# Block cross-attention into a gated FFN on one core: x kept head-major, a block-diagonal state operand, cast loads, and one batch's transpose on the DMA crossbar

## The chip, the cores and the metric

The kernel runs on one core of one Trainium2 chip. A core has a matrix engine (TensorE, PE in the profile), a vector engine (VectorE, DVE), a scalar engine (ScalarE, ACT), a general one (GpSimd, POOL) and a sync engine (SyncE, SP) that only issues transfers. Each engine executes its own instructions in order and waits for others by semaphores. Sixteen DMA engines move data. The metric is the device time of one execution in microseconds (us); lower is better.

## The reference: what is computed

For each of 8 batches and 8 heads there are 512 rows of x and 32 rows of state, 64 wide. The two attend to each other, and the result, 544 rows per batch with the heads side by side (512 wide), goes through a gated FFN with 1536 hidden units.

```
scores  = x @ state^T / 8;        a  = softmax(scores);   xread = a @ state     # 512 x 64 per head
scores2 = state @ x^T / 8;        a2 = softmax(scores2);  sread = a2 @ x        # 32 x 64 per head
z   = concat(xread, sread) per head, heads side by side                          # 4352 x 512
out = (relu(z @ w_gate) * (z @ w_val)) @ w_out                                   # 4352 x 512, f32
```

## The kernel before, in words

Work is in bf16 with f32 sums in PSUM. PSUM has eight banks of 128 x 512 f32; the program assigns them by hand.

**Folding.** xread is never formed. For each batch `u_unit` (in 512-wide pieces) or `c_unit` (in 128- or 256-wide pieces) multiplies state into w_gate and w_val (line 303), and ACT and DVE copy the products U from PSUM (313, 323). `gv` (328) multiplies U by the transposed, normalised weights `ans` and gives both FFN branches for 128 hidden units and 512 rows. ACT makes the relu of one (352), DVE multiplies it by the other (356) into h, and `out_part` (365) multiplies h by w_out. ACT copies the result out (373) and SP stores it (377). The 256 rows of sread go through `gvs` (345) at the end.

**Attention.** x of one batch lies with 128 row groups in the partitions, 4 rows (c) to each group. It is transposed so that 64-wide heads stand in partitions. A block of `xT` holds two heads of one c. State is converted into `st_b` with two copies, of which each keeps every other group of rows by a multiplication with 0 or 1 (`odd`, `state_conv`); transposed, this gives `stT`, 64 columns for each pair of heads, with each head's 32 columns zero in the other head's rows. `att_sc` (209) multiplies a block of xT by these 64 columns: 8 matmuls for four heads. Then come exp on ACT (216), sum, reciprocal and scaling on DVE (222 to 228) and a transpose to `ans`, on PE for batches 0 and 1, and by the DMA crossbar from SP for the others (`att_aT_dma`, 236). For sread the unnormalised exp is multiplied by x padded with a column of ones (`x_pad` on POOL, 265; `sr_mm`, 273).

**How x comes in and is transposed.** Four heads of batch 0 are loaded in f32 by SP and ACT and converted; its other heads, batch 1 and batch 2 are loaded by casting DMAs on POOL's queue (427, 435). [...] Batches 0 to 2 are transposed on PE: whole blocks for the converted pairs (178), and half blocks, 64 columns each, in pairs for the rest (182, 195); ACT and DVE copy the result from PSUM (186, 198). From batch 3 on, x is loaded in f32 (`x_dma`, 105; batch 3 by POOL, the rest by SP), converted by POOL in two halves (151), and transposed by the crossbar from SP (`x_trans_dma`, 168).

**Order.** Up to the fourth hidden block of batch 2 the order is a hand-written list, `program`, each word one step on each of its engines: `dx.2.0.1` loads batch 2 by a cast, `c.0.1024.256@75` is c_unit of batch 0, columns 1024 to 1279, into banks 7 and 5, `co` its copies, `gv`, `re`, `mu` are gv, relu and multiplication, `xT2.2.0`/`xo2.2.0` transposes batch 2 and copies it, `stT.1`/`sto.1` does so for the state of batches 2 and 3, `sc`, `ex`, `nr`, `nx` are the attention, `ad` the crossbar transpose of a, `o.0.1` is out_part 1 of batch 0, `do` and `ds` load w_out and state. A step of the list that a DMA queue executes waits in that queue in this order too. After the list a loop runs gv of one block and an out_part eighteen blocks behind it, and `at(b, jf, ...)` hangs the other work on blocks: loads, transposes, attention of the next batch, U of the next batch, state transposes for batches 4 to 7 by the crossbar (`state_T_dma`, copied by ACT, 138).

**Buffers.** f32 x has two buffers (`xin`), bf16 x four, xT two, output rows (`o_sb`) four. At the end `out_last` (394, 397) divides the last 128 rows into four column pieces with a copy and a store each.

Of the kernel before, what the change touches and what calls it, by code (L numbers as in the profile page):

```python
# [8 lines left out]
FP32 = mybir.dt.float32  # L9
BF16 = mybir.dt.bfloat16  # L10
# [6 lines left out]
def kernel(  # L17
# [9 lines left out]
    nc = tc.nc  # L27
# [17 lines left out]
    xin = pool("xin", 2)  # L45
# [5 lines left out]
    opool = pool("opool", 4)  # L51
# [15 lines left out]
    odd = const.tile([128, 2], FP32, name="odd")  # L67


    stT = const.tile([128, B, NJ, 64], BF16, name="stT")  # L70
# [29 lines left out]
    def x_dma(b, engs):  # L100
        xf[b] = xin.tile([128, H, NC, D], FP32, name="xf", tag="xf")
        n = H // len(engs)
        for i, eng in enumerate(engs):
            src = x[b, i * n:(i + 1) * n].rearrange("h (p c) d -> p h c d", c=NC)
            eng.dma_start(out=xf[b][:, i * n:(i + 1) * n], in_=src)

    def xb_alloc(b):
        xb[b] = att.tile([128, NC * H * D], BF16, name="xb", tag="xb", bufs=4)
# [10 lines left out]
    def state_conv(g, half, eng):  # L119
        dst, src, keep = st_b[:, g % 3, :, half], st_f[:, g], odd[:, half:half + 1]  # L120
        if eng == "act":
            nc.scalar.activation(out=dst, in_=src, func=AF.Copy, scale=keep)
        else:
            e = {"dve": nc.vector, "pool": nc.gpsimd}[eng]
            e.tensor_scalar(out=dst, in0=src, scalar1=keep, scalar2=None, op0=ALU.mult)
# [11 lines left out]
    def state_out_dma(g, eng):  # L137
        copy[eng](out=stT[:, 2 * g:2 * g + 2].rearrange("p b j m -> p (b j m)").rearrange("p (q i m) -> p q i m", i=4, m=8),
                  in_=held["st", g].rearrange("p i (q m) -> p q i m", m=8))

    def state_out(g, eng):
        copy[eng](out=stT[:, 2 * g:2 * g + 2].rearrange("p b j m -> p (b j m)"), in_=held["st", g])

    def x_conv(b, half, eng):
        if b not in xb:
            xb_alloc(b)
            xb[b] = xb[b].rearrange("p (c h d) -> p c h d", c=NC, h=H)
        conv_heads(b, slice(HK * half, HK * half + HK), eng)

    def conv_heads(b, hs, eng):  # L150
        copy[eng](out=xb[b][:, :, hs].rearrange("p c h d -> p h c d"), in_=xf[b][:, hs])  # L151

    def x_conv_pair(b, j, eng):
        dst = x_head(b)[:, :, 2 * j:2 * j + 2].rearrange("p c h d -> p h c d")
        copy[eng](out=dst, in_=xf[b][:, 2 * j:2 * j + 2])

    def x_head(b):
        return xb[b][:, 0:NC * HK * D].rearrange("p (c h d) -> p c h d", c=NC, h=HK)

    def x_tail(b):  # L160
        return xb[b][:, NC * HK * D:].rearrange("p (h c d) -> p c h d", c=NC, h=HK)

    def xT_alloc(b):
        xT[b] = att.tile([128, NC, NJ, 128], BF16, name="xT", tag="xT")

    def x_trans_dma(b):
        xT_alloc(b)
        nc.sync.dma_start_transpose(out=xT[b].rearrange("p c j t -> p (c j) t"),
                                    in_=xb[b].rearrange("p c h d -> p (c h d)"))

    def x_T(b, j):

        if b not in xT:
            xT_alloc(b)
        ps = bank("xT_ps").bitcast(BF16)[:, 0:512].rearrange("p (c t) -> p c t", c=NC)
        for c in range(NC):
            if b == 0 and j < 2:
                nc.tensor.transpose(ps[:, c], x_head(b)[:, c, 2 * j:2 * j + 2].rearrange("p h d -> p (h d)"), id128)
            else:
                v, h = (x_tail(b), 2 * j - HK) if b == 0 else (xb[b], 2 * j)  # L180
                for h2 in range(2):
                    nc.tensor.transpose(ps[64 * h2:64 * h2 + 64, c], v[:, c, h + h2], id128)  # L182
        held["xT", b, j] = ps

    def x_out(b, j, eng):
        copy[eng](out=xT[b][:, :, j], in_=held["xT", b, j])  # L186

    def x_T2(b, half):
        if b not in xT:
            xT_alloc(b)  # L190
        ps = held["xT2", b, half] = bank("xT_ps").bitcast(BF16).rearrange("p (c j t) -> p c j t", c=NC, j=2)
        for j in range(2):
            for c in range(NC):
                for h2 in range(2):
                    nc.tensor.transpose(ps[64 * h2:64 * h2 + 64, c, j], xb[b][:, c, 4 * half + 2 * j + h2], id128)  # L195

    def x_out2(b, half, eng):
        copy[eng](out=xT[b][:, :, 2 * half:2 * half + 2], in_=held["xT2", b, half])


    def att_sc(b, jp):
        if b not in e_sn:
            e_sn[b] = att.tile([128, 2, NC, NJ * Ns], BF16, name="e_sn", tag="e_sn", bufs=4)
            a_sn[b] = att.tile([128, 2, NC, NJ * Ns], BF16, name="a_sn", tag="a_sn")
        t = held["sc", b, jp] = bank("sc_ps")
        ps = t.rearrange("p (r c j n) -> p r c j n", r=2, c=NC, j=2)
        for c in range(NC):
            for jj in range(2):
                nc.tensor.matmul(ps[:, :, c, jj], xT[b][:, c, 2 * jp + jj], stT[:, b, 2 * jp + jj],  # L209
                                 start=True, stop=True)  # L210
# [49 lines left out]
    def x_pad(b):  # L260

        v = xa[:, b % NX].rearrange("p (c h) d -> p h c d", c=NC)[:, :, :, 0:D]
        for hs, src in (((0, x_head(b)), (HK, x_tail(b))) if b == 0 else ((0, xb[b]),)):
            src = src.rearrange("p c h d -> p h c d")
            nc.gpsimd.tensor_copy(out=v[:, hs:hs + src.shape[1]], in_=src)  # L265
# [31 lines left out]
    def u_mm(dst, b, w, lo, n):  # L297

        wsb = (wg_sb, wv_sb)[w]
        for j in range(NJ):  # L300
            for parity in range(2):
                r = 64 * parity
                nc.tensor.matmul(dst[parity][32 * j:32 * j + 32], stT[r:r + 64, b, j, 32 * parity:32 * parity + 32],  # L303
# [67 lines left out]
    def fin_x(b, tsub, eng="act"):  # L371
        o_sb = opool.tile([128, d_model], FP32, name="o_sb", tag="o_sb")
        copy[eng](out=o_sb, in_=held["o", b, tsub])  # L373
        n = 2 if b == B - 2 and tsub < 1 else 1
# [37 lines left out]
    xf[0] = xin.tile([128, H, NC, D], FP32, name="xf", tag="xf")  # L412
# [8 lines left out]
    nc.vector.reduce_sum(out=odd, in_=id128.rearrange("p (a h m) -> p h a m", h=2, m=8), axis=AX.XY)  # L421

    def w_load(w, lo, n):
# [3 lines left out]
    nc.gpsimd.dma_start(out=x_tail(0).rearrange("p c h d -> p h c d"),  # L427
                        in_=x[0, HK:H].rearrange("h (p c) d -> p h c d", c=NC))

    def x_load(b, part, parts):  # L430
        if part == 0:
            xb_alloc(b)
            xb[b] = xb[b].rearrange("p (h c d) -> p c h d", h=H, c=NC)
        hs = slice(H * part // parts, H * (part + 1) // parts)
        nc.gpsimd.dma_start(out=xb[b][:, :, hs].rearrange("p c h d -> p h c d"),
                            in_=x[b, hs].rearrange("h (p c) d -> p h c d", c=NC))

    def x_next(b):
        x_conv(b, 0, "pool")
        x_conv(b, 1, "pool")  # L440
        x_trans_dma(b)
# [3 lines left out]
    def spin(n, cols=512):  # L445
        for i in range(n):
# [4 lines left out]
    steps = {"spin": spin, "stc": state_conv, "stT": state_T, "sto": state_out, "xc": x_conv_pair, "xT": x_T, "xT2": x_T2, "xo2": x_out2, "on": lambda: nc.gpsimd.memset(xa[:, :, :, D:D + 1], 1.0), "dw": w_load, "dx": x_load, "ds": lambda: state_dma(nc.gpsimd, 2, B), "do": wo_dma,  # L451
             "df": lambda b: x_dma(b, (nc.gpsimd,)), "xo": x_out,
             "sc": att_sc, "ex": att_exp, "nr": att_sum, "nx": att_scale, "aT2": att_T2, "ao2": att_out2, "aT": att_T, "ao": att_out,
             "c": c_unit, "co": c_out, "u": u_unit, "uo": u_out, "gv": gv, "re": relu, "mu": mult, "o": out_part,
             "of": fin_x, "xn": x_next, "ad": att_aT_dma, "xp": x_pad, "sr": sr_mm, "sn": sr_norm}
    program = """
    dx.1.0.2 dx.1.1.2 stc.0.0.act stc.0.1.act xc.0.0.dve dw.0.0.128 spin.7 stT.0@4 xc.0.1.act dw.1.0.128 on xT.0.0@2
    sto.0.dve xT.0.1@5 xo.0.0.dve dw.0.128.128 xo.0.1.dve dw.1.128.128 spin.1 sc.0.0@3 dw.0.256.256 ex.0.0 xT.0.2@0
    xT.0.3@1 xo.0.2.dve dw.1.256.256 xo.0.3.act nr.0.0 spin.2 sc.0.1@6 dw.0.512.256 xT2.1.0@4 ex.0.1 nx.0.0
    xo2.1.0.act nr.0.1 dw.1.512.256 spin.2 xT2.1.1@2 xo2.1.1.dve sc.1.0@5 dw.0.768.256 ex.1.0 nx.0.1 dw.1.768.256  # L460
# [4 lines left out]
    ao.1.0.dve c.1.256.256@54 mu.0.1 co.0.256.256.0.act gv.1.1@21 dx.2.0.1 co.1.256.256.0.act co.0.256.256.1.dve  # L465
# [3 lines left out]
    gv.0.2@03 co.0.768.256.0.act co.1.768.256.1.dve re.0.2 gv.0.5@26 do.6.12 co.0.768.256.1.act mu.0.2 gv.1.7@41 df.3  # L469
    re.0.5 re.1.7 mu.0.5 gv.0.7@70 mu.1.7 re.0.7 gv.1.3@53 mu.0.7 re.1.3 gv.1.4@24 mu.1.3 re.1.4 gv.1.6@61 mu.1.4  # L470
    re.1.6 c.1.1280.256@70 c.0.1280.256@53 mu.1.6 co.1.1280.256.0.act c.1.1024.256@24 stc.1.0.pool xT2.2.0@6
    co.0.1280.256.0.act co.1.1024.256.0.dve xT2.2.1@1 co.0.1280.256.1.act co.1.1024.256.1.dve stc.1.1.pool
    c.0.1024.256@75 xo2.2.1.act gv.0.10@23 co.1.1280.256.1.dve stc.3.1.pool co.0.1024.256.1.dve re.0.10 gv.1.9@40
    co.0.1024.256.0.act xo2.2.0.dve stc.2.0.pool re.1.9 gv.0.6@12 mu.0.10 stc.3.0.pool re.0.6 mu.1.9 gv.0.11@57 mu.0.6
    stc.2.1.pool re.0.11 gv.0.8@64 mu.0.11 re.0.8 stT.1@3 gv.1.10@10 mu.0.8 sto.1.act re.1.10 sc.2.0@2 o.0.0@7 ex.2.0
# [115 lines left out]
```

## Time and profile before

| quantity | value |
|---|---|
| median of 3 runs | 221.95 us (221.53 to 222.31) |
| span of the profiled execution, first to last instruction | 219.9 us |
| time of the profiled execution itself | not listed apart from its span |
| granted TensorE clock, mean | 1.000 |
| HBM read / written | 18.35 / 8.91 MB, 124 GB/s over the span |
| L195 PE, half-block transposes | 64, 2.4 us busy |
| L198 ACT / DVE copies of these | 2 each, mean 1028 / 686 ns |
| L151 POOL conversions of x | 10, mean 1040 ns |
| L125 POOL conversions of state | 6, mean 915 ns |
| L138 ACT copies of crossbar-transposed state | 2, mean 622 ns |
| xf loads from SP, issue to landing | 4 of 1 MB, median 6.5 us |
| xT transposes by the crossbar, issue to landing | 5, median 5.2 us (4.3 to 6.0) |

How to read it: a row of the timeline gives the start, the time from the first to the last end of the merged instructions, engine, line, operation, output and input, and in brackets the idle time of the engine before it and what ended it. An issue row has the time from issue to landing last. In a row of the windows the last figures are the granted clock, the mean busy share of the 16 DMA engines (above 1 when transfers overlap on an engine) and the GB/s moved.

### The profile page before, as it was taken

To read this page: it belongs to the slowest core of one execution; us is meant where nothing else is said; L and a number is where in the kernel's file an instruction comes from. 1 tells how busy PE (TensorE), PEld (TensorE's weight loads), DVE (VectorE), ACT (ScalarE), POOL (GpSimd) and SP (SyncE) were. 2 spreads that over 40 slices of the span, in tenths; PEclk is the share of its full clock that TensorE was granted. 3 is DMA by queue.
4 is the path that set the end of the run, shared out by engine and by line. 5 is a ranking of instruction groups with operands and counts; after the bars stand their busy time and mean duration, and the time that the engine had idled before them with its cause. 6 is when DMAs were issued, how large, how long until landed. Compare 5 with 4: busy or idle time off the path is not lost.

```text
span 219.9 us, 4854 instructions
## 1 busy us (share of the span) xinstructions
PE 215.0 (98%) x1947; PEld 105.1 (48%) x1947; DVE 130.3 (59%) x228; ACT 124.0 (56%) x237; POOL 49.0 (22%) x54
## 2 busy tenths in 40 slices
PE   7899999999999999999999999999999999999994
PEld 3554455444444444444444444445444445666544
DVE  2697898964787569665766487648675333322100
ACT  5599887555667557555566555646654544222222
POOL 8777845360000616015000600000000000000000
PEclk9999999999999999999999999999999999999999
DMA  7999999194048593881358116701411112111132
GB/s 152 176 194 197 197 243 271 64 177 142 22 106 244 102 284 101 136 255 49 96 122 269 52 20 145 118 15 48 105 43 54 49 48 48 52 66 67 57 98 95
DMA packets 41383, 26.27 MB, mean 119 GB/s; under 512 B 22576, under 2 KB 36784, under 8 KB 41360
## 3 DMA queue, kind: packets, MB, share of 16 engines
q1 hardware_dynamic: 28496, 17.73, 31.2%
q0 software_dynamic: 11968, 7.47, 22.1%
q10 hardware_dynamic: 896, 0.75, 1.3%
q8 instruction: 15, 0.25, 0.4%
q14 instruction: 8, 0.07, 0.1%
HBM read 18.35 MB, written 8.91 MB: 124 GB/s over the span
## 4 chain that ended last, share of the span: by engine, by line
PE 94%; DMA 4%; ACT 1%; issue 0%; POOL 0%; DVE 0%; DVEq 0%; POOLq 0%
PE o_ps L365 39%; PE gv_ps L328 38%; PE gv_ps L345 5%; PE up L303 4%; DMA xb<-in_x_dram 3%; PE sc_ps L209 2%; PE upc L303 2%; PE sr_ps L273 1%; PE xT_ps L195 1%; DMA out_dram<-o_sb 1%; PE warm_ps L447 1%; PE aT_ps L244 0%; PE xT_ps L182 0%; ACT o_sb L373 0%; ACT xT L186 0%
## 5 line engine op out<-in xcount | busy, mean ns | idle before, releaser
L365 PE MATMUL o_ps<-wo_sb,h_sb 128*128 128x512 bf16 x372 | 94.6, 379 | 0.0
L328 PE MATMUL gv_ps<-ans,U 128*128 128x512 bf16 x384 | 94.1, 379 | 0.0
L356 DVE TENSOR_TENSOR h_sb<-gv_ps,g_sb 128x512 bf16<-128x512 f32 x96 | 65.2, 689 | 44.7 <-ACT g_sb L352 43.7
L352 ACT ACTIVATE g_sb<-gv_ps 128x512 bf16<-128x512 f32 (+1 forms) x108 | 63.2, 591 | 43.4 <-PE gv_ps L328 32.0
L328 PEld LDWEIGHTS <-U 128*128 128x128 bf16 x384 | 36.3, 98 | 42.2 <-issue 0.6
L365 PEld LDWEIGHTS <-h_sb 128*128 128x128 bf16 x372 | 35.4, 98 | 41.0 <-issue 2.4
L373 ACT COPY o_sb<-o_ps 128x512 f32<-128x512 f32 x31 | 18.3, 590 | 16.5 <-PE o_ps L365 16.5
L313 DVE CAST U<-up 128x512 bf16<-128x512 f32 x36 | 22.7, 684 | 5.0 <-PE up L303 5.0
L313 ACT CAST U<-up 128x512 bf16<-128x512 f32 x36 | 18.9, 594 | 11.7 <-PE up L303 11.7
L151 POOL CAST xb<-xf 128x1024 bf16<-128x1024 f32 x10 | 10.1, 1040 | 65.6 <-DMA xf<-in_x_dram 40.4
L216 ACT ACTIVATE e_sn<-sc_ps 128x512 bf16<-128x512 f32 x16 | 9.6, 599 | 11.1 <-PE sc_ps L209 11.1
L265 POOL COPY xa<-xb 128x2048 bf16<-128x2048 bf16 (+1 forms) x9 | 15.5, 1746 | 1.2 <-POOL xb L151 0.9
L356 DVE TENSOR_TENSOR hs_sb<-gv_ps,g_sb 128x256 bf16<-128x256 f32 x12 | 5.1, 425 | 15.3 <-PE gv_ps L345 10.1
L222 DVE TENSOR_REDUCE cs<-e_sn 128x16 f32<-128x512 bf16 x16 | 10.9, 680 | 4.0 <-ACT e_sn L216 4.0
L228 DVE TENSOR_TENSOR a_sn<-e_sn,rc 128x512 bf16<-128x512 bf16 x16 | 12.6, 793 | 0.4
L323 ACT CAST U<-upc 128x512 bf16<-128x512 f32 (+1 forms) x21 | 10.1, 574 | 0.5 <-PE upc L303 0.4
L303 PEld LDWEIGHTS <-stT 64*32 64x32 bf16 x512 | 5.5, 90 | 9.0 <-issue 7.6
L209 PEld LDWEIGHTS <-xT 128*128 128x128 bf16 x128 | 5.8, 99 | 4.2 <-DVE xT L186 0.8
L303 PE MATMUL up<-wg_sb,stT 64*32 64x512 bf16 x144 | 7.5, 380 | 0.0
L303 PE MATMUL up<-wv_sb,stT 64*32 64x512 bf16 x144 | 7.2, 380 | 0.0
L345 PE MATMUL gv_ps<-br,wg_sb 128*128 128x256 bf16 x48 | 7.2, 273 | 0.0
L345 PE MATMUL gv_ps<-br,wv_sb 128*128 128x256 bf16 x48 | 7.2, 273 | 0.0
(62 smaller groups left out, 116.7 us busy)
## 6 DMA issues: line engine op xcount, KB each, us to landing
out_dram<-o_sb SPq DMA_DIRECT2D x30, 256.0 KB, 2.5
xf<-in_x_dram SPq DMA_DIRECT2D x4, 1024.0 KB, 6.5
wo_sb<-in_moe_w_out_dram POOLq DMA_DIRECT2D x2, 768.0 KB, 13.6
wg_sb<-in_moe_w_gate_dram POOLq DMA_DIRECT2D x5, 256.0 KB, 8.6
wv_sb<-in_moe_w_val_dram POOLq DMA_DIRECT2D x5, 256.0 KB, 9.2
xf<-in_x_dram POOLq DMA_DIRECT2D x1, 1024.0 KB, 15.3
xb<-in_x_dram POOLq DMA_DIRECT2D x3, 256.0 KB, 6.5
xb<-in_x_dram POOLq DMA_DIRECT2D x1, 512.0 KB, 12.0
```

The source lines that it names most:

```text
L209: nc.tensor.matmul(ps[:, :, c, jj], xT[b][:, c, 2 * jp + jj], stT[:, b, 2 * jp + jj], start=True, stop=True)
L222: nc.vector.reduce_sum(out=cs, in_=e_v, axis=AX.X)
L228: {"dve": nc.vector, "pool": nc.gpsimd}[eng].tensor_tensor(out=by_pair(a_sn[b], jp).rearrange("p r (j n) -> p r j n", n=Ns), in0=e_v, in1= ...
L265: nc.gpsimd.tensor_copy(out=v[:, hs:hs + src.shape[1]], in_=src)
L303: nc.tensor.matmul(dst[parity][32 * j:32 * j + 32], stT[r:r + 64, b, j, 32 * parity:32 * parity + 32], wsb[r:r + 64, j, lo:lo + n], start= ...
L313: copy[eng](out=U[b][:, w, kc, lo:lo + 512], in_=held["u", b, w, lo][kc])
L328: nc.tensor.matmul(ps[w], U[b][:, w, kc, f0:f0 + 128], ANS[b][:, kc].rearrange("p c t -> p (c t)"), start=(kc == 0), stop=(kc == NK - 1))
L345: nc.tensor.matmul(ps[w][:, 0:nt], wsb[:, j, f0:f0 + 128], br[:, j].rearrange("p b n -> p (b n)"), start=(j == 0), stop=(j == NJ - 1))
L352: nc.scalar.activation(out=g_sb[:, 0:n], in_=ps[0][:, 0:n], func=AF.Relu)
L356: nc.vector.tensor_tensor(out=dst, in0=ps[1][:, 0:n], in1=held["g", b, jf][:, 0:n], op=ALU.mult)
L365: nc.tensor.matmul(held["o", b, tsub], src[:, jf, tsub * 128:(tsub + 1) * 128], wo_sb[:, jf], start=(jf == 0), stop=(jf == NF - 1))
L373: copy[eng](out=o_sb, in_=held["o", b, tsub])
```

## The change

- bf16 x of every batch is now head-major (head, c, d). A block to be transposed is one head with two of its rows c (128 wide), so that every transpose is a whole one: 16 on PE for batch 0 and 16 for batch 1, instead of 8 whole and 48 half ones.
- `stT` has 64 columns for each head: the head's 32 columns in the upper half of the partitions and again, as columns 32 to 63, in the lower half; the rest is zeroed once by a DVE memset. `att_sc` still has 8 matmuls of 64 columns for four heads. State is copied twice without a mask, and each transposed state is copied out in two half-partition copies, for batches 0 to 3 one on ACT and one on DVE, for the others both on POOL.
- Batch 2's transposes leave PE with their copies: `xd.2` issues a crossbar transpose on SP, in the list directly behind the load.
- Batches 3 to 7 are loaded by cast DMAs on POOL's queue; the f32 loads and the POOL conversions go. f32 x has one buffer of half the size.
- `o_sb` has eight buffers; one more store of batch 6 is divided in two.

```diff
-    xin = pool("xin", 2)
+    xin = pool("xin", 1)
-    opool = pool("opool", 4)
+    opool = pool("opool", 8)
...
-    stT = const.tile([128, B, NJ, 64], BF16, name="stT")
+    stT = const.tile([128, B, H, 64], BF16, name="stT")
...
     def state_conv(g, half, eng):
-        dst, src, keep = st_b[:, g % 3, :, half], st_f[:, g], odd[:, half:half + 1]
...
+        copy[eng](out=st_b[:, g % 3, :, half], in_=st_f[:, g])
...
+    def state_dst(g, half):
+        return stT[64 * half:64 * half + 64, 2 * g:2 * g + 2, :, Ns * half:Ns * half + Ns]
+    def state_out(g, half, eng):
+        rows = slice(64 * half, 64 * half + 64)
+        copy[eng](out=state_dst(g, half).rearrange("p b h n -> p (b h) n"),
+                  in_=held["st", g][rows].rearrange("p (q n) -> p q n", n=Ns))
...
+    def x_blocks(b):
+        return xb[b].rearrange("p h (k c) d -> p (h k) (c d)", c=2)
     def x_trans_dma(b):
         xT_alloc(b)
-        nc.sync.dma_start_transpose(out=xT[b].rearrange("p c j t -> p (c j) t"),
-                                    in_=xb[b].rearrange("p c h d -> p (c h d)"))
+        nc.sync.dma_start_transpose(out=xT[b], in_=xb[b].rearrange("p h c d -> p (h c d)"))
+    def x_T(b, lo, n):
...
+        for k in range(n):
+            nc.tensor.transpose(ps[:, k], x_blocks(b)[:, lo + k], id128)
...
-        for c in range(NC):
-            for jj in range(2):
-                nc.tensor.matmul(ps[:, :, c, jj], xT[b][:, c, 2 * jp + jj], stT[:, b, 2 * jp + jj],
+        for h in range(4 * jp, 4 * jp + 4):
+            for k in range(2):
+                nc.tensor.matmul(ps[:, h % 2, 2 * k:2 * k + 2, h // 2 % 2], xT[b][:, 2 * h + k], stT[:, b, h],
...
-        n = 2 if b == B - 2 and tsub < 1 else 1
+        n = 2 if b == B - 2 and tsub < 2 else 1
...
     nc.vector.memset(warm, 0.0)
+    nc.vector.memset(stT, 0.0)
...
 program (words that differ)
-    sto.0.dve ... xT2.1.0@4 xo2.1.0.act ... xT2.1.1@2 xo2.1.1.dve
+    sto.0.0.dve sto.0.1.act ... xT.1.0.8@4 xo.1.0.8.act ... xT.1.8.8@2 xo.1.8.8.dve
-    gv.1.1@21 dx.2.0.1 co.1.256.256.0.act
+    gv.1.1@21 dx.2.0.1 xd.2 co.1.256.256.0.act
-    gv.1.7@41 df.3
+    gv.1.7@41 dx.3.0.1
-    c.1.1024.256@24 stc.1.0.pool xT2.2.0@6 ... xT2.2.1@1 ... xo2.2.1.act ... xo2.2.0.dve
+    c.1.1024.256@24 stc.1.0.pool
-    stT.1@3 gv.1.10@10 mu.0.8 sto.1.act re.1.10 sc.2.0@2
+    stT.1@3 gv.1.10@10 mu.0.8 sto.1.0.act sto.1.1.dve re.1.10 sc.2.0@2
-    nr.2.1 xn.3 re.1.11
+    nr.2.1 xd.3 re.1.11
...
-    at(2, 6, x_dma, 4, (nc.sync,))
+    at(2, 6, x_load, 4, 0, 1)
-        at(2, 8 + g, state_out_dma, g, "act")
+        at(2, 8 + g, state_out_dma, g, 0, "pool")
+        at(2, 8 + g, state_out_dma, g, 1, "pool")
-            at(s, 9, x_next, b + 1)
+            at(s, 9, x_trans_dma, b + 1)
-            at(s, 10, x_dma, b + 2, (nc.sync,))
+            at(s, 10, x_load, b + 2, 0, 1)
```

## The prediction, made before the changed kernel was run

> **What bounds the kernel now.** I read the busy line first, then the slices, then the chain that ended last.
>
> ```profile
> PE 215.0 (98%) x1947; PEld 105.1 (48%) x1947; DVE 130.3 (59%) x228; ACT 124.0 (56%) x237; POOL 49.0 (22%) x54
> PE   7899999999999999999999999999999999999994
> DMA  7999999194048593881358116701411112111132
> PE 94%; DMA 4%; ACT 1%; issue 0%; POOL 0%; DVE 0%; DVEq 0%; POOLq 0%
> ```
>
> TensorE (PE) sets the time from about 13 us on; the granted clock is full in every slice. So time can be won by taking work off PE or by shortening its waits, and there is little of either: 219.9 - 215.0 = 4.9 us of idle PE, most of it in the first and last slices. The DMA row matters as much for this change: the 16 DMA engines are full until about 39 us, and the change puts a new transfer into that stretch.
>
> The only PE work removed is in the timeline of 29 to 38 us:
>
> ```profile
> 29.86 0.29 PE L303 MATMUL upc<-wg_sb,stT 64*32 64x256 bf16 x8
> 29.88 1.56 ACT L323 CAST U<-upc 128x512 bf16<-128x512 f32 x3 [0.20 <-PE upc L303]
> 30.19 1.08 PE L195 MATMUL xT_ps<-id,xb 128*64 128x128 bf16 x32
> 31.20 0.30 PE L303 MATMUL upc<-wg_sb,stT 64*32 64x256 bf16 x8
> 31.55 4.49 PE L328 MATMUL gv_ps<-ans,U 128*128 128x512 bf16 x20
> ...
> 36.27 0.69 DVE L356 TENSOR_TENSOR h_sb<-gv_ps,g_sb 128x512 bf16<-128x512 f32 x1 [0.17 <-PE stT_ps L130]
> 36.30 0.58 ACT L142 COPY stT<-stT_ps 128x512 bf16<-128x512 bf16 x1
> ...
> 36.96 0.40 PE L209 MATMUL sc_ps<-stT,xT 128*128 128x64 bf16 x8
> 37.19 1.03 PE L365 MATMUL o_ps<-wo_sb,h_sb 128*128 128x512 bf16 x4
> ```
>
> The 32 transposes of batch 2 (L195) hold PE from 30.19 to 31.20. What stands on either side of them are c units (L303), whose PSUM banks ACT empties meanwhile. The later lines show `stT.1`'s copy on ACT ending at 36.88, just before the scores of batch 2 start.
>
> **Start, cost 0 (bounds -0.15 and +0.15).** Batches 0 and 1 lose 48 half-width transposes and gain 24 whole ones. That is no saving: two halves run side by side. 16 halves took 0.64 us (at 9.20), 8 whole ones 0.62 (L244 at 12.33). What is waited for there are the landings of x on the POOL queue, at 7.53 and 10.28, and those DMAs stay as they are. The new zeroing of `stT` on DVE is eight times the first memset (0.27 us): 2.2 us, from 1.1 to 3.3, under DVE's wait for xf until 4.02. If it ran 0.7 us over, it would eat into the wait for 7.53, which has room.
>
> **Batch 2's transposes leave PE: -0.24, not -1.01.** The next PE work is c.0.1024, which goes to banks 7 and 5. Bank 5 holds the first half of c.0.1280, and ACT's three casts (29.88 to 31.44, 0.52 apart) empty it with the second, at 30.92. So PE, free at 30.08, waits until about 30.96 and starts c.0.1024 there instead of at 31.20. The first gv then starts 0.24 earlier; its second matmul needs the third cast (31.44), in time. The transposes were cover for the casts. The copies they leave to ACT (1.04 at 31.32) and DVE (0.68 at 32.72) delayed no PE work: the 20 gv matmuls ran without a gap. Bounds: 0 and -1.01.
>
> **`stT.1` is copied out in two halves: +0.48.** `sto.1.1.dve` comes behind `mu.0.8` on DVE, which runs 36.27 to 36.96 because it waits for its relu on ACT. DVE copied the first `stT` (L142) in 0.42 us, so this half ends at 37.38, and the scores of batch 2, which need both halves, start near 37.44 instead of 36.96. Queued behind them on PE is everything else. Nothing hides this: PE executes in order. Bounds: 0 (DVE gets there early) and +0.75 (the strided half at the 0.68 of an f32 cast, L323).
>
> **The crossbar transposes batch 2: +0.30.** This is the uncertain term. The transfers:
>
> ```profile
> xb<-in_x_dram POOLq DMA_DIRECT2D x1, 512.0 KB, 12.0
> wo_sb<-in_moe_w_out_dram POOLq DMA_DIRECT2D x1, 768.0 KB, 14.0
> ...
> wo_sb<-in_moe_w_out_dram POOLq DMA_DIRECT2D x1, 768.0 KB, 13.2
> xT<-xb SPq DMA_TRANSPOSE x5, 5.2
> ```
>
> Batch 2's x is issued at 17.41 and lands at 29.42; the two halves of w_out are issued at 20.07 and 24.75 and land at 34.07 and 37.95. Their consumers: batch 2's scores (36.96), the first o part (37.19) and the third matmul of the second o part, which needs the second half of w_out at 39.15 + 0.43 = 39.58. The windows show how full the engines are then, and what a transpose moves when alone (last row):
>
> ```profile
> 30.00:31.00 1.00, 1.00 (x54) 0.81 (x32) 1.00 (x3) 1.00 (x3) 0.50 (x1) 1.00 1.28 221
> 36.00:37.00 1.00, 1.00 (x11) 0.53 (x9) 0.79 (x2) 0.94 (x3) 0.00 (x0) 1.00 1.20 313
> 39.00:40.00 1.00, 1.00 (x6) 0.43 (x5) 0.97 (x2) 0.57 (x2) 0.00 (x0) 1.00 0.43 152
> 45.00:46.00 1.00, 1.00 (x7) 0.44 (x5) 1.00 (x2) 0.13 (x1) 1.00 (x2) 1.00 1.17 212
> ```
>
> At 212 GB/s (last figure of a row) 512 KB take 2.45 us. The quickest of the five xT transposes landed 4.3 us after its issue, so 1.85 lie around the data. SP has nothing ahead of it and issues at 29.42. With the engines shared half and half the data take 4.9: landing at 29.42 + 1.85 + 4.9 = 36.2, before 37.44, no wait. But everything on the POOL queue comes up to 2.45 later: the second half of w_out at 40.40, while PE asks for it at 39.58 - 0.24 + 0.48 = 39.82, a wait of 0.58. If the transpose's SBUF traffic fits beside HBM-bound loads, the wait is 0. I take the middle, 0.30. The far bound is in the rivals. Batch 3's load as a cast changes little here: 512 KB written at 196 GB/s is 2.7 us, the plain 1 MB at 370 was 2.8.
>
> [...]
>
> **Later x by cast loads, cost 0.** Ten POOL casts of 1.04 us go; POOL was 22% busy. Batch 4's load moves from SP (64.1) to POOL, right behind batch 3's pad (about 47.6), so it is early. Batch 5's stands behind batch 4's pad, which waits for the sr of batch 2 (about 70), and behind two `stT` copies: issue about 73 (before: 74.9), landing at 85 even at 12 us, and its transpose sits at 89. Loads 6 and 7 have more room. On SP, each transpose no longer waits for POOL; what is behind it there (outputs, the small sn transposes) gets earlier. ad.2 stays behind batch 3's transpose: if that load lands 2.45 later than 40.87, ans of batch 2 comes near 50.2 against 49.7, and is wanted at 51.4. If this cover went, PE would wait for the difference. The four POOL copies of `stT` take two copies of 0.62 off ACT, which PE does not wait for.
>
> [...] In this trace a POOL issue beside DVE's two-input bf16 multiply (9.13) took 0.74 us, no more than the others; if an issue were late by 3 us, the slack above would take it and the sum stays.
>
> **Tail: -0.16.** With eight output buffers the last copy need not wait:
>
> ```profile
> 216.76 0.23 DVE L397 COPY o_sb<-o_ps 128x64 f32<-128x64 f32 x1 [10.54 <-PE o_ps L394]
> 217.22 0.23 DVE L397 COPY o_sb<-o_ps 128x64 f32<-128x64 f32 x1 [0.23 <-DMA out_dram<-o_sb]
> ```
>
> PE's last matmul ends at 217.02, so the copy could start at 217.06. The additional split output of batch 6 is far from the end. Bounds: 0 and -0.2.
>
> **Sum.** -0.24 + 0.48 + 0.30 - 0.16 = +0.38 on a span of 219.9. The median of the runs is 221.95, 2.05 above the span; I take that as constant: 222.3 us. A measurement tells about 0.3% (0.67 us) from no change, so this is no change.
>
> **Rivals.**
> - *PE's removed work is paid in full.* For it: PE is the bound, and the c units' banks might be empty sooner than the merged ACT row says. Against it: that row ends at 31.44. -1.01 and -0.16, with the split copy and the crossbar hidden: 220.8. Chance 0.20.
> - *The transpose starves* (slower). Place: batch 2's scores on PE, which stand in front of all that follows. It decides once xT of batch 2 lands after 37.44, 8.0 us after its source. If the transpose gets what the POOL queue leaves, it ends when all is moved: the loads end at 39.4, plus 2.45, plus 0.6 to land (a third of the 1.85): 42.45. Against 36.96 that is +5.5; the split copy and w_out hide in it; with the tail +5.3: 227.3. Half-way, 224.6. For it: a DMA share above 1 throughout, and a backlog of w_out and x. Against it: the first x loads on SP and ACT's queues landed in 3.3 and 3.5 us while POOL's took 6.1. Chance 0.27.
> - *It does nothing:* both small costs and both gains vanish, 221.9. This lies within the main case.
>
> **Numbers.** Main case, 221.3 to 223.2, chance 0.53: of it 0.36 within 0.3%, 0.15 slower, 0.02 faster. Rival one: 0.19 faster, 0.01 within. Rival two: all slower. Together faster 0.21, same 0.37, slower 0.42. The range goes from 220.7 (rival one) to 225.5 (somewhat over half-way of rival two): it leaves out about 0.05 below and 0.12 above.
>
> **What would show it.** Removal: c.0.1024 right behind c.1.1024 with a PE gap near 0.9 us ended by an ACT cast. Split copy: PE's idle before batch 2's scores ended by DVE's `stT` copy near 37.4. Crossbar: the time to landing of the first xT transpose, 6.8 in the main case, 13 in the second rival, and whether PE idles before the scores or the second o part. Tail: no DVE idle ended by an output DMA. I would be wrong if the start moved by more than 0.15 us, or if a later batch's scores waited for xT.

## The result, and the profile after

| quantity | before | after |
|---|---|---|
| median, 4 runs each | 222.13 us (221.53 to 222.65) | 233.86 us (232.85 to 234.43) |
| ratio | | 1.0506, 95% interval 1.0447 to 1.0564 |
| span of the profiled execution | 219.9 us | 232.6 us (its time 234.43) |
| mean granted TensorE clock | 1.000 | 0.975 |
| POOL busy | 49.0 us | 40.7 us |

The change makes the kernel about 5% slower; the forecast was 222.3 us with a range up to 225.5. Five lines of the page of the changed kernel answer to those shown of before: busy time, PE's slices, the granted clock and the DMA share in the same 40 slices (5.8 us each), and the shares of the chain that ended last.

```profile
PE 216.6 (93%) x1891; PEld 105.2 (45%) x1891; DVE 130.3 (56%) x228; ACT 122.9 (53%) x235; POOL 40.7 (17%) x51
PE   7799994299999999999999999999999999999991
PEclk9999999569999999999999999999999999999998
DMA  6999999747885698367336113611311112211132
PE 87%; DMA 10%; POOL 1%; issue 0%; DVE 0%; POOLq 0%
```

PE was full from 13 us on; now two slices, from 34.9 to 46.5, are half empty or more, and in two, from 40.7 to 52.3, the clock is down. The chain's DMA share has risen from 4% to 10%. The page's list of that chain names it: `DMA xT<-xb 6%`. The PE timeline shows the place (idle time before a row and what ended it in brackets):

```profile
30.95 0.27 PE L262 MATMUL upc<-wg_sb,stT 64*32 64x256 bf16 x1 [0.26 <-ACT U L282]
31.44 0.30 PE L262 MATMUL upc<-wg_sb,stT 64*32 64x256 bf16 x7 [0.22 <-ACT U L282]
...
31.78 4.49 PE L287 MATMUL gv_ps<-ans,U 128*128 128x512 bf16 x20
...
36.33 1.03 PE L287 MATMUL gv_ps<-ans,U 128*128 128x512 bf16 x4
45.27 0.61 PE L170 MATMUL sc_ps<-stT,xT 128*128 128x64 bf16 x8 [7.91 <-DMA xT<-xb]
45.69 1.89 PE L324 MATMUL o_ps<-wo_sb,h_sb 128*128 128x512 bf16 x4
```

The row of 45.27 is the heart of the case: batch 2's scores wait 7.91 us for the crossbar transpose. The row under it has a second cost. Four matmuls of `out_part` take 1.89 us where the same row before took 1.03. The SP timeline has the issue (start, time that it held SP):

```profile
30.51 7.25 SPq L148 DMA_TRANSPOSE xT<-xb  x1
```

The view of the tile xT has the shortest, median and longest time from issue to landing of its six crossbar transposes:

```profile
DMA to landing us min/median/max: 4.3/4.9/14.7
```

The 14.7 is batch 2's. The others move as many bytes; the quickest took 4.3 and the median is 4.9. One of them, issued at 77.47 beside a cast load of 512 KB, took 8.25. The windows of the changed kernel (the last three figures are the granted clock, the DMA share and GB/s):

```profile
34.00:35.00 1.00, 1.00 (x6) 0.44 (x5) 0.80 (x2) 0.60 (x1) 0.00 (x0) 1.00 1.21 196
39.00:40.00 1.00, 0.00 (x0) 0.00 (x0) 0.00 (x0) 0.00 (x0) 0.00 (x0) 1.00 1.09 115
40.00:41.00 1.00, 0.00 (x0) 0.00 (x0) 0.00 (x0) 0.00 (x0) 0.00 (x0) 0.64 1.34 183
45.00:46.00 1.00, 0.73 (x9) 0.55 (x10) 0.00 (x0) 0.09 (x1) 0.00 (x0) 0.50 0.00 0
50.00:51.00 1.00, 1.00 (x5) 0.43 (x4) 1.00 (x2) 0.00 (x0) 0.00 (x0) 0.74 0.00 0
51.00:52.00 1.00, 1.00 (x7) 0.44 (x5) 0.36 (x2) 0.50 (x1) 0.00 (x0) 1.00 0.00 0
```

The DMA engines are full until after 42. The clock halves inside the microsecond from 40: a mean of 0.64 between 1 and 0.5 puts the change at 40.3, 2.9 us after PE's last work (36.33 + 1.03 = 37.36). The 0.74 puts the return to full clock at 50.5, 5.2 us after work resumed.

**The account.** Differences of PE start times, after less before, in the profiled executions:

| up to | sum so far | this step |
|---|---|---|
| first gv (13.97, before 13.49) | +0.48 | +0.48, the start |
| gv.0.10 (31.78, before 31.55) | +0.23 | -0.25, batch 2's transposes gone |
| batch 2's scores (45.27, before 36.96) | +8.31 | +8.08, the wait |
| last group of matmuls (224.86, before 214.18) | +10.68 | +2.37, work at half clock |
| last DVE copy ends (227.96, before 217.45) | +10.51 | -0.17, no wait for a buffer |
| end of the span | +12.7 | +2.2: the last store lands 1.7 later after that copy, and what follows it takes 0.5 more |

From 55 us on the difference stands at 10.68 up to the last group, so the five later batches cost nothing more.

### The profile page after: what moved, and what is told of

It reads as the page before. It is cut to its first block, busy times and chain, and to the rows that moved or that the text cites. A ratio compares the mean times of both kernels' runs of the same rounds, so it can differ in the third digit from the quotient of the medians.

```text
span 232.6 us, 4728 instructions
## 1 busy us (share of the span) xinstructions
PE 216.6 (93%) x1891; PEld 105.2 (45%) x1891; DVE 130.3 (56%) x228; ACT 122.9 (53%) x235; POOL 40.7 (17%) x51
## 4 chain that ended last, share of the span: by engine, by line
PE 87%; DMA 10%; POOL 1%; issue 0%; DVE 0%; POOLq 0%
PE o_ps L324 38%; PE gv_ps L287 34%; DMA xT<-xb 6%; PE gv_ps L304 5%; PE up L262 4%; DMA xb<-in_x_dram 3%; PE sc_ps L170 2%; PE upc L262 1%; PE sr_ps L232 1%; PE o_ps L353 1%; PE aT_ps L205 0%; POOL xb L386 0%; POOL xb L392 0%; PE warm_ps L398 0%; PE xT_ps L156 0%
## 5 line engine op out<-in xcount | busy, mean ns | idle before, releaser
L324 PE MATMUL o_ps<-wo_sb,h_sb 128*128 128x512 bf16 x372 | 96.0, 384 | 0.0
L224 POOL COPY xa<-xb 128x2048 bf16<-128x2048 bf16 x8 | 15.1, 1901 | 78.5 <-PE sr_ps L232 53.0
L170 PE MATMUL sc_ps<-stT,xT 128*128 128x64 bf16 x128 | 7.2, 199 | 8.0 <-DMA xT<-xb 7.9
L189 DVE TENSOR_TENSOR a_sn<-e_sn,rc 128x512 bf16<-128x512 bf16 x16 | 10.9, 685 | 0.4
```

The source lines that it names most:

```text
L170: nc.tensor.matmul(ps[:, h % 2, 2 * k:2 * k + 2, h // 2 % 2], xT[b][:, 2 * h + k], stT[:, b, h], start=True, stop=True)
L189: {"dve": nc.vector, "pool": nc.gpsimd}[eng].tensor_tensor(out=by_pair(a_sn[b], jp).rearrange("p r (j n) -> p r j n", n=Ns), in0=e_v, in1= ...
L224: nc.gpsimd.tensor_copy(out=v, in_=xb[b])
L324: nc.tensor.matmul(held["o", b, tsub], src[:, jf, tsub * 128:(tsub + 1) * 128], wo_sb[:, jf], start=(jf == 0), stop=(jf == NF - 1))
```

## The theories and the experiments

- **A.** The transpose is slow because it shares the DMA engines with the POOL queue, where both halves of w_out and batch 3's load are under way; PE's idle time then halves its clock.
- **B.** It is slow here by itself, whatever else is moved.
- **C.** The cast loads and the new state operand cost several us of their own.

Ratios are to the kernel before, run on the same chip beside each group.

**1. Batch 2 back on PE, all else as changed.**

```diff
-gv.1.1@21 dx.2.0.1 xd.2 co.1.256.256.0.act
+gv.1.1@21 dx.2.0.1 co.1.256.256.0.act
+ ... xT.2.0.8@6 ... xT.2.8.8@1 ... xo.2.8.8.act ... xo.2.0.8.dve
```

> The changed kernel with one part undone: batch 2 is transposed on PE again (16 whole transposes and two copies in the old places), and the crossbar transpose behind its load goes. Theory A (that crossbar transpose shares the DMA engines record by record with the POOL queue's loads of w_out and batch 3, lands at 45.2 instead of near 37, PE idles 7.9 us and then runs 5 us at half clock): PE no longer waits before batch 2's scores except for the split state copy (about 0.5), the clock stays full, and the time is 222.5 to 224. Theory B (a crossbar transpose at this place is slow by itself, whatever else is moved): the same here. Theory C (the cast loads or the new state operand cost several us elsewhere): 226 or more.

Measured: 223.85 us, ratio 1.0039 (0.9998 to 1.008). Theory C is out: without `xd.2` nearly everything is gone. What is left shows in the PE timeline as `[0.35 <-DVE stT L134]` before the scores: the split state copy.

**2. Batch 3's load only after the transpose has landed** (a small POOL copy that reads xT stands ahead of it).

```diff
-gv.1.7@41 dx.3.0.1
+gv.1.7@41
-stc.2.1.pool re.0.11
+stc.2.1.pool gate.2 dx.3.0.1 re.0.11
```

> The changed kernel, but batch 3's cast load is issued only after batch 2's crossbar transpose has landed (a small POOL copy that reads its output stands ahead of the load). The transpose then shares with w_out alone. Theory A: w_out ends near 38, the rest of the transpose runs alone, it lands near 40 to 41 instead of 45.2, PE idles 3 to 4 us, the clock hardly drops, 226 to 229. Theory B: time to landing stays near 14.7, 233 to 234.5.

Measured: 230.55 us, ratio 1.034 (1.0277 to 1.0403). Expected were 226 to 229 and a clock that hardly drops; it was at half for 6.83 us, from 39.11. The transpose was issued at 29.05 and landed about 11.2 us later instead of 14.7. PE timeline:

```profile
40.34 0.61 PE L170 MATMUL sc_ps<-stT,xT 128*128 128x64 bf16 x8 [4.15 <-DMA xT<-xb]
```

The wait falls from 7.91 to 4.15, the time to landing by 3.5: so much had the load cost that was taken away. w_out is still there, so this is only half of theory A.

**3. PE kept busy while it waits**, by 34 matmuls whose result nobody reads.

```diff
-sto.1.1.dve re.1.10 sc.2.0@2
+sto.1.1.dve re.1.10 hot.34@7 sc.2.0@2
```

> The changed kernel with 34 additional 128x512 matmuls on PE ahead of batch 2's scores (7.3 us, results unused), so that PE is busy while the transpose is under way. Theory A with the half clock as a price of its own: the wait ends at the same 45 us, but the granted clock stays 1.0 and the work up to 51 us runs at full speed: 2.3 to 2.6 us less than the changed kernel, about 231.4. If the half clock were only a mark of idleness and cost nothing: 233.9.

Measured: 230.13 us, ratio 1.0316 (1.0259 to 1.0374), clock 1.000. PE timeline:

```profile
37.19 7.50 PE L405 MATMUL hot_ps<-hs_sb 128*128 128x512 bf16 x33
45.31 0.41 PE L170 MATMUL sc_ps<-stT,xT 128*128 128x64 bf16 x8 [0.61 <-DMA xT<-xb]
45.55 1.03 PE L324 MATMUL o_ps<-wo_sb,h_sb 128*128 128x512 bf16 x4
```

The scores start where they started in the changed kernel (45.31, there 45.27), but `out_part` takes 1.03 again, and the last group of matmuls starts at 222.37 instead of 224.86. The clock had thus cost 2.5 us on PE. The spans of the two profiled executions differ by 4.2 (228.5, 232.6), as do the two ratios; the other 1.7 lies behind the last copy, where this kernel needs 3.0 us to the end and the changed one 4.7 (below).

**4. The transpose beside PE's own**, into a buffer that nobody reads (kernel of 1, plus one transpose on SP; six output buffers).

```diff
-gv.1.1@21 dx.2.0.1 co.1.256.256.0.act
+gv.1.1@21 dx.2.0.1 xdd.2 co.1.256.256.0.act
```

> The kernel of the first run plus the crossbar transpose of batch 2 at its place, into a buffer that nothing reads (and six output buffers for room). It shows what the transpose costs the loads, without PE waiting for it. Theory A: it still takes 12 to 15 us to land although PE is busy; the second half of w_out lands 1.5 to 2.5 us later than in the first run, and PE waits 0.3 to 1.2 us for it in the second o part: 0.3 to 1.2 us over the first run. If the loads were not slowed: within 0.2 us of the first run.

Measured: 223.3 us, ratio 1.0027 (0.999 to 1.0064). The view of the unread tile has the time to landing:

```profile
DMA to landing us min/median/max: 15.7/15.7/15.7
```

Two rows of the PE timeline of the same kernel have what PE waits for around it:

```profile
37.51 0.39 PE L170 MATMUL sc_ps<-stT,xT 128*128 128x64 bf16 x8 [0.35 <-DVE stT L134]
...
40.48 0.59 PE L324 MATMUL o_ps<-wo_sb,h_sb 128*128 128x512 bf16 x2 [0.18 <-DMA wo_sb<-in_moe_w_out_dram]
```

It takes 15.7 us with PE at work, so PE's idleness doesn't cause the slowness. To other transfers it is cheap: the second half of w_out takes 15.7 instead of the 13.0 of experiment 1, and PE waits 0.18 for it, less than the 0.3 to 1.2 expected. Nearly all of the change's cost is that somebody waits for the transpose.

**5. w_out and batch 3's load all behind the landing** (the gate of 2, with both `do` steps behind it too).

```diff
-mu.1.0 do.0.6 ... gv.0.5@26 do.6.12 ... gv.1.7@41 dx.3.0.1
+mu.1.0 ... gv.0.5@26 ... gv.1.7@41
-stc.2.1.pool re.0.11
+stc.2.1.pool gate.2 do.0.6 do.6.12 dx.3.0.1 re.0.11
```

> The changed kernel with both halves of w_out and batch 3's load issued only when the transpose of batch 2 has landed (a small POOL copy reads it). Theory A (the POOL queue's loads take every second record): with none of them the transpose lands 4.5 to 6 us after its issue near 30, at 35 to 36, and the scores of batch 2 do not wait for it; the wait moves to the first o part, for w_out, which can land near 41 to 42 at the earliest: 3.5 to 5 us of idle there, median 226 to 230. Theory B (the transpose is slow in this place by itself): it lands 12 or more us after its issue, the scores wait 5 us or more and the o part after them again: over 236.

Measured: 231.6 us, ratio 1.0403 (1.0379 to 1.0428). The issue on SP was at 29.75. In the POOL timeline the small copy starts when the transpose has landed:

```profile
34.80 0.21 POOL L404 COPY mark<-xT 128x16 bf16<-128x16 bf16 x1 [1.94 <-DMA xT<-xb]
```

The PE timeline of the same kernel has the new wait:

```profile
37.22 0.39 PE L170 MATMUL sc_ps<-stT,xT 128*128 128x64 bf16 x8 [0.35 <-DVE stT L134]
42.29 1.86 PE L324 MATMUL o_ps<-wo_sb,h_sb 128*128 128x512 bf16 x4 [4.68 <-DMA wo_sb<-in_moe_w_out_dram]
```

The copy starts 5.05 us after the issue: in the same place, with the POOL queue empty, the transpose is as quick as later ones. Theory B is out. And the wait has only moved, to w_out, where 4.68 us halve the clock again (1.86); that price was not in the 226 to 230 expected. In this stretch the transfer that comes last is waited for, in either order.

**6. Batch 2's load and transpose two weight pieces earlier.**

```diff
-gv.0.0@14
+gv.0.0@14 dx.2.0.1 xd.2
-gv.1.1@21 dx.2.0.1 xd.2 co.1.256.256.0.act
+gv.1.1@21 co.1.256.256.0.act
```

> The changed kernel with batch 2's load (and its crossbar transpose) two weight pieces earlier in the queues. The load should land near 28 instead of 30.5. If the transpose gets every second record while the POOL queue is loaded, it lands a constant 14 to 15 us after its issue: near 42.7, the idle before batch 2's scores falls from 7.9 to 5 to 6 us, median 230.5 to 232. If it gets only what the POOL queue leaves and so ends with the backlog, it lands near 45 as before: median 233 to 234.5. The weight pieces behind it may make the last c units wait up to 1 us.

Measured: 233.14 us, ratio 1.048 (1.0457 to 1.0504). The issue was 3.7 us earlier (26.84), the landing only 1.1 (17.3 us after the issue). PE timeline:

```profile
44.18 0.61 PE L170 MATMUL sc_ps<-stT,xT 128*128 128x64 bf16 x8 [7.34 <-DMA xT<-xb]
```

My constant of 14 to 15 us from issue to landing is wrong, and by its time the run went as "ends with the backlog" said. Which of the two holds can be read from the transfer records of the trace, counted by their start per microsecond, on all 16 engines, for the POOL queue and SP's queue:

| kernel, stretch | POOL queue's records | transpose's records (256 bytes) |
|---|---|---|
| changed, 33 to 34 | 193 of 1024 bytes | 0 |
| changed, 35 to 36 | 153 of 1024 bytes | 147 |
| changed, 40 to 41 | 233 of 512 and 3 of 1024 bytes | 238 |
| changed, 42 to 43 | 117 of 512 bytes | 426 |
| experiment 6, 31 to 32 | 152 of 1024 bytes | 149 |
| experiment 6, 41 to 42 | 238 of 512 bytes | 237 |
| experiment 5, 33 to 34 | 0 | 1133 |

From 35 to 41 in the changed kernel the counts of a microsecond differ by 8% at most; in sum they are 1057 for the POOL queue and 1066 for the transpose. So while both queues had work, one moved about as many records as the other. (Whether they alternate one by one or in equal handfuls the counts do not show.) From 41 on the counts are no longer equal, 225 against 279 and then 117 against 426; the POOL queue is near its end there (its last record starts at 44.5). The transpose does not live on leftovers. But a record of w_out lasts 96 ns and one of the transpose 31 ns (medians), so equal counts gave the transpose 31 of 127 ns, a quarter of the time, and a fifth of the bytes. It has 2048 records (512 KB in 256 bytes). When the transpose's first record moves, the POOL queue has about 2220 of the 2560 records of w_out and batch 3's load left in experiment 6, and about 1530 in the changed kernel. So the transpose ends near the end of that backlog in both, and an earlier start buys little: more of its partners are then the slow records of w_out (1194, against 502).

**7. The state copy of batches 2 and 3 earlier** (kernel of 1).

```diff
-re.0.11 gv.0.8@64 mu.0.11 re.0.8 stT.1@3 gv.1.10@10 mu.0.8 sto.1.0.act sto.1.1.dve re.1.10
+re.0.11 stT.1@3 gv.0.8@64 mu.0.11 sto.1.1.dve re.0.8 gv.1.10@10 sto.1.0.act mu.0.8 re.1.10
```

> Batch 2 is transposed on PE again; stT.1 is transposed one gv earlier and its DVE half stands ahead of mu.0.8, so that batch 2's scores should wait for neither copy. Theory A (the split copy costs 0.35 to 0.5 us through its place behind mu.0.8 on DVE): the idle of 0.35 before the scores goes, the scores start 0.4 to 0.5 earlier against the first gv than with PE transposes alone, median ratio to before 1.000 to 1.002. Theory C (the new operand costs something elsewhere): the ratio stays at 1.003 to 1.004.

Measured: 223.21 us, ratio 1.0017 (1.000 to 1.0035). The idle of 0.35 before the scores is gone from the PE timeline:

```profile
37.77 0.39 PE L170 MATMUL sc_ps<-stT,xT 128*128 128x64 bf16 x8
```

From gv.0.10 to the scores it is 5.68 us; it was 5.92 in 1 and 5.41 before. Half of the half microsecond comes back, not all of it as expected. The other 0.27 stands in the ACT timeline of the same kernel:

```profile
37.14 0.58 ACT L134 COPY stT<-stT_ps 64x512 bf16<-64x512 bf16 x1
```

ACT's half of the copy now ends last, at 37.72, and the scores start 0.05 behind it.

**8. Only a quarter of the zeroing at the start** (kernel of 7; the rest of `stT` zeroed by POOL later).

```diff
-    nc.vector.memset(stT, 0.0)
+    nc.vector.memset(stT[:, 0:2], 0.0)
+    ... "zr": lambda: nc.gpsimd.memset(stT[:, 2:], 0.0)
```

> The last kernel, with stT of batches 0 and 1 alone zeroed at the start (a quarter of the memset), the rest by POOL later. If the long memset on DVE delays the cast loads of x at the start, the first half of batch 0 lands 0.2 to 0.4 us earlier than in the last kernel and the ratio is 0.999 to 1.000. If the start is late for another reason or only varies, landings and ratio stay as in the last kernel within 0.002.

Measured: 222.86 us, ratio 1.0022 (0.9993 to 1.005). In its profile the first gv starts at 13.19, 0.88 earlier than in 7, but the ratio doesn't move. The profile of 7 has half clock from 7.35 to 10.77 and this one none, so the 0.88 can't be put down to the memset. This kernel and that of 7 are the best forms of the change that I found. Neither beats the kernel before.

**9. The kernel before, once more.**

> The kernel before once more, unchanged, to see how much its start and its tail vary from one profile to another. If the start of the changed kernel is late because of its memset, the first two PE transposes of cast-loaded x (7.57 and 10.30 before) come at the same times here within 0.1; if the landings only vary, they move by 0.2 to 0.9. The stretch from the end of the last DVE copy to the end of the span was 2.45; if the tail varies by chance it may be 3 to 4.6 here as well.

Measured: 221.85 us. The first two PE transposes of cast-loaded x for which PE can wait start at 7.39 and 10.47 (7.57 and 10.30), the first gv at 13.71 (13.49). The last DVE copy ends at 217.63 and the span at 220.1: 2.5 us, as before. So the tail of before repeats, and its start varies by 0.2.

**10. The kernel of 8 with four output buffers.**

```diff
-    opool = pool("opool", 8)
+    opool = pool("opool", 4)
```

> The kernel with a quarter of the memset and batch 2 on PE, with four output buffers instead of eight. If the eight buffers give what the prediction says, the last DVE copy waits 0.2 to 0.25 for a store again, ends 3.27 instead of 3.10 after the start of the last PE group, and the median rises by 0.1 to 0.2, too little to tell from no change. If eight buffers lengthen the tail by crowding the last stores, the median falls by 0.5 or more.

Measured: 224.11 us, ratio 1.0071 (1.004 to 1.0102), by the ratios 1.1 us above the kernel of 8 (which ran on another chip), where 0.1 to 0.2 was expected. Its DVE timeline at the end:

```profile
218.62 0.22 DVE L356 COPY o_sb<-o_ps 128x64 f32<-128x64 f32 x1 [10.54 <-PE o_ps L353]
219.90 0.23 DVE L356 COPY o_sb<-o_ps 128x64 f32<-128x64 f32 x1 [1.06 <-DMA out_dram<-o_sb]
```

The wait for a buffer is 1.06 here, where the kernel before had 0.23: the store that frees it took 2.9 us to land, there 2.06. With eight buffers the two copies run as one row of 0.57. The eight buffers thus save this wait, whatever its length. The start also differs in this profile, though not by the edit: cast-loaded x is waited for 1.75 us, the clock is at half from 7.94 to 11.36, and the first gv starts at 15.11. That is not all of the difference: among the executions with a mean clock of 0.996 or more, the median is 223.66 here (before, on the same chip, 222.09) and 222.55 in 8 (before 222.37).

**11. The changed kernel, once more.**

> The changed kernel once more, unchanged. If the transpose's landing is set by turns with the POOL queue, it lands 14 to 15.5 us after its issue again. If the late last store comes from an instruction fetch that falls by chance on the last stores, its 3.2 us may be 1.5 to 2 here; if it belongs to the kernel, it is 3 or more again.

Measured: 232.0 us. Issue 28.90, landing 14.9 us later, idle 7.51; the last two 32 KB stores took 3.2 and 3.05 us to land. The first gv starts at 12.88, earlier than in either profile of before.

## Why the prediction was wrong, step by step

- **Failed: "The crossbar transposes batch 2: +0.30".** The step read "with the engines shared half and half the data take 4.9: landing at 29.42 + 1.85 + 4.9 = 36.2". Shared half and half were the records, not the time. The issue came 1.1 later (30.51) and the landing was at 45.2: 14.7 us in place of 1.85 + 4.9. Two things make the difference. The first record of the transpose moved only 4.0 us after the issue (in experiment 5: 1.3), and why is not shown. And then the 2048 records took 10.2 us (in experiment 5: 3.25), beside records of up to three times their duration (96 ns against 31).
- **The equal shares on which that sum rests: no run shows them.** What the runs showed in their place are equal counts of records, 147 against 153: a fifth of the bytes for the transpose, and beside w_out's records a quarter of the time (31 of 127 ns).
- **The same step, on w_out: right in kind, the landing in part by luck.** I had the second half of w_out landing at 40.40 and a price of 0 to 0.58. (That the loads are bound by HBM, as the case with price 0 had it, no run shows.) It landed at 40.6 (25.14 + 15.5), but in the second profile of the changed kernel at 39.25. From issue to landing it took 15.0 to 16.6 us in the six profiles in which a transpose shared the engines, and 13.0 to 14.0 without one (before twice, experiments 1 and 7). In experiment 4, where nobody waits for the transpose, PE waits 0.18 for it. The POOL queue was slowed about as forecast; the other side of the sharing was wrong.
- **Rival two, "The transpose starves" (0.27, 227.3): right in place, sign and condition, too small.** It gave 42.45 for the landing, with the transpose taking what is left over. It moved as many records as that queue instead, 1066 beside 1057 from 35 to 41, and started late. And no case of mine had the price of an idle PE afterwards: 1.5 to 2.6 us at half clock in the five profiles with a long wait (change of the difference to before between the wait's end and the last group of matmuls: 2.37 and 1.46 in the changed kernel's two, 2.56 in experiment 2, 2.22 in 5, 2.47 in 6; -0.16 in 3, where PE was kept busy).
- **"Batch 2's transposes leave PE: -0.24": right.** -0.25. In place of one gap near 0.9 there are two of 0.26 and 0.22 with a matmul between them; both are ended by ACT's casts, as described. Experiment 5 repeats it: gv.0.10 starts 17.85 after the first gv, before 18.06.
- **"`stT.1` is copied out in two halves: +0.48": right, once it can be seen.** In the changed kernel the long wait hides it. In experiments 1, 4 and 5 the scores start 5.92 to 5.93 us after gv.0.10, before 5.41: +0.5.
- **"Start, cost 0 (bounds -0.15 and +0.15)": neither shown nor refuted.** The profiled +0.48 is outside the bounds, but two profiles of the changed kernel differ by 1.1 at the first gv (13.97, 12.88) and the kernels with a quarter of the memset by 1.9 (13.19, 15.11). The memset took 1.76 us, from 1.50 to 3.26, and DVE waited for xf until 3.92. The seven profiles with the whole memset and full clock at the start lie from 12.80 to 13.97, around the 13.49 and 13.71 of before, so no cost of the memset shows. The bounds were too narrow for one profile.
- **"Later x by cast loads, cost 0": right.** PE waits for no later batch, and the difference to before is the same 10.68 at 55 us and at 225.
- **"Tail: -0.16": right for the copy (-0.17), but not all of the tail.** After the last copy the changed kernel needs 4.7 us to the end, before 2.45. Its last two DMA issues on ACT take 2.37 us together instead of 1.19, and the last 32 KB stores land in 3.2 to 3.3 us instead of 1.5. In the trace a 16 KB transfer of the instruction queue lasts 1.7 us at that moment. Such transfers come 12 to 24 us apart late in these profiles, and in the four profiles in which one began beside or after the last issues (the changed kernel twice, experiments 5 and 6) the last stores took about 3 us. In experiment 2, with a transfer just behind the issues, they did too. In before and experiment 8 it came ahead of them, and they took 1.5 to 1.8. This is a coincidence in time that I saw and did not test. Another 0.5 of the tail passes behind the last landing.

So of +12.7 us in the span, 8.1 are the wait (shown by experiments 1, 2 and 5), 2.4 the clock (shown by 3), 2.2 the last stores and what follows them (seen, not tested), and the small terms cancel.

## What to carry to other kernels

Before you move work from an engine to a DMA, look at whether the DMA engines are full between its source and its consumer; if they are, count records and not bytes: here two queues moved about equal numbers of records (1057 and 1066 in six microseconds), and the one with the small records got a quarter of the time beside w_out's (31 of 127 ns). Price the consumer's wait first and the slowed neighbours second, and add the slower clock when TensorE would stand idle for long (waits of 4.15 to 7.91 us halved it here and cost 1.5 to 2.6 us more). Transposes that leave TensorE are worth only what TensorE did not need as cover: here 0.25 of 1.01 us.

## What the runs showed of the hardware that was not expected

- **Equal counts of records.** 147 records of 256 bytes beside 153 of 1024 in a microsecond, 237 beside 238 of 512. Alone the transpose reached 1133 in a microsecond.
- **A late first record.** Beside a full POOL queue the transpose's first record moved 4.0 us after its issue (3.95 to 3.99 in six profiles), and SP was held for 6.6 to 8.6 us by that one issue; with the queue empty it was 1.3 us and 3.1.
- **The clock.** Up to the last change, the stretches of one clock in the records last whole multiples of 3.41 us: 34.13, 10.24 and 180.91 in the changed kernel, 215.04 in the kernel before. The stretches at half clock lasted 3.41 us (at the start of experiments 7 and 10), 6.83 or 10.24. The changed kernel paid 2.37 us in the profile with 10.24 at half clock and 1.46 in the one with 6.83. In the five profiles with a long wait the cost is 0.43 to 0.46 of the time from the wait's end to the return of the clock. The clock went down 2.5 to 4.1 us after PE's last work and up 3.4 to 5.6 after its next began (times in us below).

| profile | PE idle | half clock | its length | cost |
|---|---|---|---|---|
| changed | 37.36 to 45.27 | 40.27 to 50.51 | 10.24 | 2.37 |
| changed, again | 36.38 to 43.89 | 40.44 to 47.27 | 6.83 | 1.46 |
| experiment 2 | 36.19 to 40.34 | 39.11 to 45.94 | 6.83 | 2.56 |
| experiment 5 | 37.61 to 42.29 | 40.39 to 47.21 | 6.83 | 2.22 |
| experiment 6 | 36.84 to 44.18 | 39.36 to 49.60 | 10.24 | 2.47 |

- **The start.** The first gv of the same kernel began at 12.88 and at 13.97 (the changed kernel), so a single profile does not tell half a microsecond there. The three latest of all thirteen profiles (experiments 1, 7 and 10: 14.54, 14.07, 15.11) are those with one step of half clock between 7.3 and 11.4; the waits of PE just before it were 0.35 to 1.75 us. Whether the step makes them late, or the waits make both, is not shown.
- **Instruction transfers.** 16 KB, 12 to 24 us apart in the last 80 us, which lie beside the last stores in some kernels and not in others.
